# A refitted static order, DMAs begun from ScalarE's queue, and a rebuilt end in an FFT, MLP and soft-MoE kernel

## Chip, cores and metric

One Trainium2 chip, one core. The metric is the device time of one execution in microseconds; three runs of the kernel before took 1426.42, 1427.17 and 1430.96 us, median 1427.17.

## What is computed

Input `x` is 8 batches of 3072 tokens by 256 numbers, float32. Cut to what matters:

```python
X = np.fft.fft(np.fft.fft(x, axis=1), axis=2).real      # per batch, 3072 x 256
h = X.reshape(-1, 256) @ w_in                           # 256 -> 2048
y = (h - np.tanh(h)) @ w_out                            # 2048 -> 256
logits = y @ phi                                        # 32 slots, all 24576 tokens
d = softmax(logits, axis=0)                             # over the tokens
slot_in = d.T @ y                                       # 32 x 256
slot_out = [relu(slot_in[e] @ w1[e]) @ w2[e] for e in range(8)]   # 4 slots an expert
out = softmax(logits, axis=1) @ slot_out                # 24576 x 256
```

The softmax over tokens needs every token's logits, so no output can be written before the last batch is through: the kernel has a loop over the input and then an end, in which the experts run and 25.17 MB of output are made and stored.

## The kernel before

**Loop.** A batch is 12 tiles, and a tile is 4 groups of 512 of the 2048 hidden columns: 96 tiles, 384 groups. For each batch a part of the Fourier transform over tokens is done by additions on 128x1024 pieces of `x` (`dft24`, additions at L327, on GpSimd but for the first batch, scalings at L331 on ScalarE). These run while the batch before goes through the rest, so the loads of batch b (`load_x`, L306, eight DMAs a batch) have to come a batch ahead. For each tile `z_dft` (L411 to L414) finishes the transform on TensorE. For each group, in this order: `wide` (L462) makes two results `pp` and `qq` with three matmuls each, called a pass here; `evac` (L476) and `plus` (L481) on VectorE and `minus` (L484) on GpSimd put them together to h of two mirrored rows; ScalarE makes tanh (`act_h`, L489) and a scaled half-precision copy (`act_t`, L497); VectorE makes the low half (`low_t`, L501); a DMA transposes both (`turn_t`, L505), issued by SyncE (SP); TensorE multiplies the transposed pieces `tt` to `logits` (L532, 16 matmuls) and the untransposed ones to `slots` (L640, 24 matmuls a tile). Every two tiles `ls_sum` (L544) makes logits, which `ls_keep` (L551, SP) stores to `lsd` in DRAM for the end, and a running softmax scales what is summed in `acc` (`acc_add`, L644).

**What sets the order.** Class `Flow` (L112) is a list planner that runs when the program is built. Every operation is entered with a cost on its engine (V VectorE, A ScalarE, G GpSimd, T TensorE, D the DMA queue of SP), what it reads and writes, and the ring of buffers that it takes or frees; the planner then fixes one order for each engine. Entries are sorted by a due place, which `SCHED` gives for every kind of operation in groups (L46), and an engine looks at the next 40 of its entries. The transposes are entered with 2.4 on SP and 2.0 more until they land:

```python
        put(g + 0.001, {"D": 2.4}, lambda e, g=g: turn_t(g), [("t1", g, 0), ("t1", g, 1)], [("tt", g)], "tt", "", 2.0, "low_t1")
```

On the chip nothing is reordered: an engine that waits for a semaphore holds all that is behind it, and a DMA is issued in its place in the instruction stream of the engine that starts it. Before, SP starts all of them.

**Head.** `w_in` and `w_out` come as raw 64-bit halves in 16 pieces of 512 KB (`load_w`, L760). VectorE puts each together in six steps, the last one an addition (`join`, L797). When all are there `top_1` (L884, reduction at L886) finds the largest of w_out times phi, whose scale everything behind needs.

**End.** `late` constants and weights: `wo_unit` (L1055), `wl_unit` (L1067, w1 of experts 6 and 7), `lt_unit` (L1062, logits of four batches), `w128_unit` (L1073, constants `ct` and `wwd`), `t_unit` (L1080, w2, into the ring `tr` of the transposes' sources, 16 DMAs at L1050). Then the sum is normalized (`norm`, `a_norm`), `slot_in` (L1337), the experts' `up` (L1375) and `down` (L1388), `place` and `placed` to `R`; and for each batch a softmax of its logits (`c_max` to `c_div`, L1447 to L1464), twelve transposes `c_t`, twelve products `mix` (L1514), copies to an output buffer `mixed` (L1410 on VectorE, L1412 on ScalarE), and stores.

Of the kernel before, what the change touches and what calls it, by code (L numbers as in the profile page):

```python
# [9 lines left out]
F32 = mybir.dt.float32  # L10
# [216 lines left out]
def fft_mlp_softmoe_kernel(ctx: ExitStack, tc: tile.TileContext, x, w_in, w_out, phi, w1, w2, cq, fd, cm, ct, out):  # L227
# [67 lines left out]
    def load_x(b, cgs=(0, 1), sets=(0, 1, 2)):  # L295
        xb = xbs[b % 2]
        xr = x[b].rearrange("(j p) d -> p j d", p=128)
        for cg in cgs:
            for a in sets:
                c = 4 * cg  # L300
                while c < 4 * cg + 4:
# [4 lines left out]
                    ny.dma_start(out=xb[:, 8 * a + c:8 * a + c + n, :], in_=xr[:, j:j + 3 * (n - 1) + 1:3, :])  # L306
# [3 lines left out]
    tA = tmp.tile([128, 4, 256], F32, name="tA")  # L310
    tB = tmp.tile([128, 4, 256], F32, name="tB")
# [448 lines left out]
    def load_w(dst, src, a, u):  # L760
# [828 lines left out]
```

## Time and profile before

| | us |
|---|---|
| runs | 1426.42, 1427.17, 1430.96 |
| profiled execution | 1421.73 |
| its span on the core | 1419.9 |
| TensorE busy | 1284.0 (90% of the span) |
| VectorE busy | 1241.7 (87%) |
| ScalarE busy | 1132.4 (80%) |
| GpSimd busy | 1126.9 (79%) |
| chain that ended last: DMA `tt<-tr` | 28% |

The span runs from the first to the last instruction of the core; the profiled execution's own time has 1.8 us around it. Shares of busy time are means over head, loop and end, so they are read by stretch. The chain that ended last is followed back from the last instruction, at each step to what released it.

### The profile page before, as it was taken

The numbers are of one execution on the slowest core, as the hardware profiler recorded it, in microseconds if no ns is written. First come the engines' busy times: TensorE is split into PE (matmuls) and PEld (weight loads), VectorE is DVE, ScalarE is ACT, GpSimd is POOL, SyncE is SP. The second block draws the span as 40 slices with busy tenths as digits, with TensorE's granted clock in tenths as the row PEclk, the third lists the DMA queues.
The fourth block names the chain that finished last, engine by engine and source line by source line (L and its number), as shares of the span: only waits on it lengthen the run. The fifth ranks groups of instructions, "written<-read, shape, count | busy, mean of one in ns | idle before, by whom it ended". The sixth has DMA issues, their size and how long they took to land.

```text
span 1419.9 us, 37237 instructions
## 1 busy us (share of the span) xinstructions
PE 1284.0 (90%) x14062; PEld 936.3 (66%) x14062; DVE 1241.7 (87%) x2233; ACT 1132.4 (80%) x2522; POOL 1126.9 (79%) x864
## 2 busy tenths in 40 slices
PE   3889999999899999999999999899989999995886
PEld 2666776667676766677776677676767667762464
DVE  7989898989999999999999999899989989992572
ACT  3459887988888888888898889788988888881476
POOL 5957898999999999999999999899999964430420
PEclk9999999999999999999999999999999999996998
DMA  7469999999999999999999999999999999999778
GB/s 237 149 184 201 200 189 190 180 200 182 207 198 182 196 200 198 188 193 198 207 198 185 194 206 191 188 189 204 185 197 194 213 193 203 189 205 309 238 316 372
DMA packets 856867, 292.84 MB, mean 206 GB/s; under 512 B 803440, under 2 KB 847344, under 8 KB 854896
## 3 DMA queue, kind: packets, MB, share of 16 engines
q1 hardware_dynamic: 856688, 290.47, 104.1%
q8 instruction: 110, 1.80, 0.5%
q14 instruction: 69, 0.57, 0.1%
HBM read 58.15 MB, written 30.67 MB: 63 GB/s over the span
## 4 chain that ended last, share of the span: by engine, by line
PE 58%; DMA 30%; DVE 5%; POOL 2%; issue 2%; ACT 2%; SPq 0%; DVEq 0%; ACTq 0%
DMA tt<-tr 28%; PE pp L462 13%; PE qq L462 12%; PE L L532 9%; PE ta L640 8%; PE op L1514 3%; POOL h L484 1%; PE L L525 1%; PE zps L411 1%; PE zps L412 1%; PE zps L413 1%; PE zps L414 1%; PE hps L838 1%; PE tps L450 1%; PE L L526 1%
## 5 line engine op out<-in xcount | busy, mean ns | idle before, releaser
L484 POOL TENSOR_TENSOR h<-pb,h 128x512 f32<-128x512 f32 x384 | 493.7, 1289 | 146.3 <-DVE h L481 120.8
L489 ACT ACTIVATE th<-h 128x512 f32<-128x512 f32 x768 | 462.2, 613 | 96.8 <-DVE h L481 72.5
L501 DVE SCALAR_TENSOR_TENSOR tr<-th,tr 128x512 f16<-128x512 f32 x768 | 510.5, 682 | 3.2 <-ACT tr L497 3.0
L497 ACT ACTIVATE tr<-th 128x512 f16<-128x512 f32 x768 | 446.0, 607 | 6.7 <-issue 1.3
L462 PE MATMUL pp<-Wh,zh 128*128 128x512 f32 x768 | 335.6, 437 | 0.1
L462 PE MATMUL qq<-Wh,zh 128*128 128x512 f32 x768 | 329.9, 430 | 0.1
L476 DVE SCALAR_TENSOR_TENSOR pb<-W,zts,pp 128x512 f32<-128x512 f32 x384 | 284.3, 741 | 40.9 <-PE pp L462 37.8
L532 PE MATMUL L<-WPn,tt 128*128 128x64 f16 (+1 forms) x6144 | 231.0, 185 | 67.8 <-DMA tt<-tr 66.5
L532 PEld LDWEIGHTS <-tt 128*128 128x128 f16 x6144 | 194.4, 96 | 144.4 <-DMA tt<-tr 105.6
L481 DVE SCALAR_TENSOR_TENSOR h<-pb,qq 128x512 f32<-128x512 f32 x384 | 260.3, 678 | 15.0 <-PE qq L462 6.8
L462 PEld LDWEIGHTS qq<-Wh,zh 128*128 128x128 f32 x768 | 146.2, 190 | 55.6 <-issue 9.1
L462 PEld LDWEIGHTS pp<-Wh,zh 128*128 128x128 f32 x768 | 148.9, 194 | 20.8 <-DVE pb L476 0.7
L327 POOL TENSOR_TENSOR xb<-xb 128x508 f32<-128x508 f32 (+3 forms) x102 | 144.0, 1423 | 18.5 <-DVE xb L327 14.1
L462 PE MATMUL qq<-Wl,zh 128*128 128x512 f32 x384 | 153.5, 400 | 0.0
L462 PE MATMUL pp<-Wl,zh 128*128 128x512 f32 x384 | 152.5, 397 | 0.0
L640 PE MATMUL ta<-tr,dh 128*32 128x512 f16 x2304 | 145.9, 390 | 0.0
L327 POOL TENSOR_TENSOR tA<-xb 128x1024 f32<-128x1024 f32 (+2 forms) x70 | 106.2, 1522 | 1.6 <-ACT xb L331 1.2
L640 PEld LDWEIGHTS <-dh 128*32 128x32 f16 x2304 | 55.9, 98 | 72.1 <-issue 23.4
L327 POOL TENSOR_TENSOR xb<-tA 128x508 f32<-128x508 f32 (+2 forms) x79 | 83.5, 1063 | 0.1
L327 POOL TENSOR_TENSOR xb<-xb,tA 128x512 f32<-128x512 f32 (+1 forms) x46 | 75.9, 1651 | 9.3 <-DVE xb L327 8.6
L462 PEld LDWEIGHTS qq<-Wl,zh 128*128 128x128 f32 x384 | 74.0, 193 | 5.6
L462 PEld LDWEIGHTS pp<-Wl,zh 128*128 128x128 f32 x384 | 73.9, 192 | 1.3
(256 smaller groups left out, 1886.2 us busy)
## 6 DMA issues: line engine op xcount, KB each, us to landing
out<-xb SPq DMA_DIRECT2D x14, 1536.0 KB, 5.4
xb<-in_x SPq DMA_DIRECT2D x32, 512.0 KB, 5.3
tr<-in_moe_w SPq DMA_DIRECT2D x16, 512.0 KB, 9.5
tt<-tr SPq DMA_TRANSPOSE x385, 5.0
xb<-in_moe_w SPq DMA_DIRECT2D x12, 512.0 KB, 4.7
raw<-in_moe_w_in SPq DMA_DIRECT2D x8, 512.0 KB, 4.2
xb<-in_x SPq DMA_DIRECT2D x16, 256.0 KB, 4.1
raw<-in_moe_w_out SPq DMA_DIRECT2D x8, 512.0 KB, 3.6
```

The lines of the kernel that those rows point to most:

```text
L327: fn = lambda e: e.tensor_tensor(out=out[1](), in0=a[1](), in1=c[1](), op=op)
L411: nt.matmul(zps[:, 0, :], xb[:, U, 0:128], C, start=True, stop=False)
L462: nt.matmul(o, z, v, start=n == 0, stop=n == 2)
L476: nv.scalar_tensor_tensor(out=pb, in0=W128[:, c, :], scalar=zs[i][3][:, 129:130], in1=pqs.pop((g, 0)), op0=ALU.mult, op1=ALU.add)
L481: nv.scalar_tensor_tensor(out=hs[g][:, 0, :], in0=pbs[g], scalar=0.5, in1=pqs.pop((g, 1)), op0=ALU.mult, op1=ALU.add)
L484: ng.tensor_tensor(out=hs[g][:, 1, :], in0=pbs.pop(g), in1=hs[g][:, 0, :], op=ALU.subtract)
L489: ns.activation(out=o, in_=hs[g][:, k, :], func=AF.Tanh)
L497: ns.activation(out=place_t(g)[:, 0, k], in_=ths[g, k], func=AF.Copy, scale=T14)
L501: nv.scalar_tensor_tensor(out=t[:, 1, k], in0=ths.pop((g, k)), scalar=T14, in1=t[:, 0, k], op0=ALU.mult, op1=ALU.subtract)
L532: nt.matmul(L[:, pm].rearrange("p b s -> p (b s)")[:, 0:n], tt[:, hl, pm, f, :], WPn[:, 4 * c + f].rearrange("p b s -> p (b s)")[:, 0:n], ...
L640: nt.matmul(tas[p][32 * c:32 * c + 32, :], dhl[p][:, dl, 2 * k + pm, :], ts[c][:, tl, pm, :], start=(k == 0 and n == 0), stop=(i == tiles( ...
L1514: nt.matmul(o.rearrange("p r d -> p (r d)"), c[:, j, :], R[:, 3 * h + k:3 * h + k + 2, :].rearrange("p r d -> p (r d)"), start=(h == 0), s ...
```

## The change

It has four parts.

**Order of the loop.** The due places are other numbers; a transpose is entered with 2.8 and 2.4 instead of 2.4 and 2.0.

**Queues.** The loads of `x` for batches 1 to 7 and the 48 stores of logits are started by ScalarE (`ns`) and not by SP (`ny`). `soft_e` no longer waits for the store, but for the last pair.

**Head.** Eight of the 16 `join`s, those of `w_out` (`apart`), run on GpSimd; the first part of `dft24(0)` runs on GpSimd alone; the loads stand in another order.

**End.** `tA` and `tB`, the scratch of `dft24`, come from the pool of weights and take the constants `ct` and `wwd` when the last transform is done (`const_unit`). w1 of experts 6 and 7 go where `cqs` and `Wl` were. Of the logits only batch 0's are loaded ahead of w2, the softmax of batch 0 is done in the main flow, batches 1 to 3 are loaded behind w2. The sum is not normalized ahead of `slot_in`, but its result is scaled when it is copied to `si`. Products take one of 8 banks each (`room`). `R` is made from PSUM straight. Output buffers are four (two of `xbs`, two pieces of `tr`) where they were two, and the planner gets a tolerance for lateness for each operation of the end (`TL`), and starts from the state in which the main flow ends.

```diff
-DSTEPS = 22.767
-XLEAD = -9.594
-XSTEP = -9.498
-XEARLY = 39.387
-XFIRST = 9.894
+DSTEPS = 12.326
+XLEAD = 6.384
+XSTEP = 1.383
+XEARLY = 15.709
+XFIRST = 26.17
 SCHED = {
-    "soft_t": 14.318, "logits": 5.085, "slots": 17.012, "soft_d": 14.96, "z_slots": 17.04, "z_turn": -1.424,
+    "soft_t": 13.814, "logits": 5.849, "slots": 16.458, "soft_d": 14.952, "z_slots": 17.162, "z_turn": -0.253,
...
-                    ny.dma_start(out=xb[:, 8 * a + c:8 * a + c + n, :], in_=xr[:, j:j + 3 * (n - 1) + 1:3, :])
+                    (ns if b else ny).dma_start(out=xb[:, 8 * a + c:8 * a + c + n, :], in_=xr[:, j:j + 3 * (n - 1) + 1:3, :])
...
     def ls_keep(p):
         b, n = divmod(2 * p, NQ)
-        ny.dma_start(out=lsd_of(b)[:, 2 * n:2 * n + 4, :], in_=lsw[p])
+        ns.dma_start(out=lsd_of(b)[:, 2 * n:2 * n + 4, :], in_=lsw[p])
...
         def join(_):
-            nv.tensor_tensor(out=vf, in0=vf, in1=Y.pop(("f", u)), op=ALU.add)
+            f, lo = Y.pop(("f", u)), tt_.pop(u)[:, :, 0]
+            if u in apart:
+                ng.tensor_tensor(out=vf, in0=vf, in1=lo.bitcast(F32), op=ALU.add)
+            else:
+                nv.tensor_tensor(out=vf, in0=vf, in1=f, op=ALU.add)
...
+    tt_, apart = {}, {("wo", c, k) for c in range(4) for k in range(2)}
...
-    x_part(1)
     hf.add({"D": 1.0}, load_fd, w=["fds"], lat=2.0)
     hf.add({"A": 0.6}, start, ["fds", "cms"], ["fdz"])
-    w_units(units[1:2])
+    w_units(units[1:3])
+    x_part(1)
+    w_units(units[3:5])
     x_part(0)
-    w_units(units[2:])
+    w_units(units[5:])
...
-            hf.add({"V": 0.15 + 0.267 * n, "G": 0.19 + 0.55 * n}, lambda e, fn=fn: fn(vg[e]), r, w, port="V")
+            hf.add({"G": 0.17 + 0.53 * n}, lambda e, fn=fn: fn(vg[e]), r, w)
...
-            put(p0 - XEARLY + 3 * n if n < 3 else p0 + XSTEP * (n - 3), {"D": 1.1}, lambda e, b=b, cg=cg, a=a: load_x(b, (cg,), (a,)), (), ks, "", "",
-                3.5, late=LATES.get("XLEAD", 0.0))
+            put(p0 - XEARLY + 3 * n if n < 3 else p0 + XSTEP * (n - 3), {"A": 0.65}, lambda e, b=b, cg=cg, a=a: load_x(b, (cg,), (a,)), (), ks, "", "",
+                5.0, late=LATES.get("XLEAD", 0.0))
...
-        put(g + 0.001, {"D": 2.4}, lambda e, g=g: turn_t(g), [("t1", g, 0), ("t1", g, 1)], [("tt", g)], "tt", "", 2.0, "low_t1")
+        put(g + 0.001, {"D": 2.8}, lambda e, g=g: turn_t(g), [("t1", g, 0), ("t1", g, 1)], [("tt", g)], "tt", "", 2.4, "low_t1")
...
-        put(8 * p, {"D": 0.75}, lambda e, p=p: ls_keep(p), [("ls", p)], [("lk", p)], "", "", 2.0, "ls_keep")
+        put(8 * p, {"A": 0.4}, lambda e, p=p: ls_keep(p), [("ls", p)], [("lk", p)], "", "", 2.0, "ls_keep")
...
+    early = [(wo_unit, (k,), 1.38) for k in range(4)] + [(lt_unit, (0,), 1.0), (w7_unit, (1,), 1.38)]
+    early += [(w1_part, (6, 0), 1.38), (w1_part, (6, 1), 1.38), (w7_unit, (0,), 1.38)]
...
-    fl = Flow({"cs": 2, "ct": 2, "o": 4, "t": 2, "ot": 2})
+    fm = fl
+    fl = Flow({"cs": 2, "ct": 2, "B": 8, "ot": 4}, 80)
...
-    fl.add({"A": 0.4}, lambda _: ns.copy(out=si, in_=X.pop("b")), ["sip"], ["si"])
+    fl.add({"A": 0.4}, lambda _: ns.activation(out=si, in_=X.pop("b"), func=AF.Copy, scale=rs), ["sip", "rs"], ["si"], free="B:sip")
...
+    for b in range(1, NL):
+        fl.add({"D": 1.0}, lambda _, b=b: lt_unit(b), ["w2s"], [("l", b)], lat=2.0)
...
+    ots = [*xbs, *(tr[:, k:k + 6, :].bitcast(F32).rearrange("p a (b d) -> p (a b) d", d=256) for k in (1, 9))]
...
-            X["ot", b] = xbs[b % 2]
+            X["ot", b] = ots[b % 4]
```

**SP in the loop, before** (L505 is the transpose, L306 a load of x, L551 a store of logits):

```order
L505 DMA_TRANSPOSE tt<-tr 128x16x128 x2
L306 DMA xb_75<-in_x 128x3x256
L306 DMA xb_75<-in_x 128x256
L306 DMA xb_75<-in_x 128x4x256
L505 DMA_TRANSPOSE tt<-tr 128x16x128 x5
L306 DMA xb_75<-in_x 128x4x256
L505 DMA_TRANSPOSE tt<-tr 128x16x128
L551 DMA lsd_57<-lsw 128x128
L505 DMA_TRANSPOSE tt<-tr 128x16x128 x8
```

In the changed program SP has `L508 DMA_TRANSPOSE tt<-tr 128x16x128 x299` there in one row, with no other DMA between. What left it stands on ScalarE, between tanh (L492) and scaled copies (L500), **ScalarE in the loop, after**:

```order
L500 ACTIVATE tr<-th 128x512
L492 ACTIVATE th<-h 128x512
L434 COPY z_4703<-zps 128x256
L492 ACTIVATE th<-h 128x512
L500 ACTIVATE tr<-th 128x512
L310 DMA xb_76<-in_x 128x4x256
L500 ACTIVATE tr<-th 128x512
L457 COPY zts<-tps 128x256
L492 ACTIVATE th<-h 128x512
```

The load stands between two halves of `act_t`; before, ScalarE's order held no DMA.

**TensorE around the logits of group 101, before.** The pass on `qq_6462` is the second of group 106, `tt` is group 101's transpose:

```order
L462 MATMUL qq_6462<-Wh_84,zh_6225 128x512
L462 MATMUL qq_6462<-Wl_85,zh_6225 128x512
L462 MATMUL qq_6462<-Wh_84,zh_6225 128x512
L532 LDWEIGHTS tt_6319
L532 MATMUL L_6174<-WPn_114,tt_6319 128x64
```

Logits follow the pass at once.

**TensorE there, after**, where the same pass writes `qq_6451`:

```order
L465 MATMUL qq_6451<-Wh_84,zh_6240 128x512
L465 MATMUL qq_6451<-Wl_85,zh_6240 128x512
L465 MATMUL qq_6451<-Wh_84,zh_6240 128x512
L414 MATMUL zps_6461<-cqs_113,xb0_75 128x128
L415 MATMUL zps_6461<-cqs_113,xb0_75 128x128
L416 MATMUL zps_6461<-cqs_113,xb0_75 128x128
L417 MATMUL zps_6461<-cqs_113,xb0_75 128x128
L465 MATMUL pp_6471<-Wh_84,zh_6240 128x512
L465 MATMUL pp_6471<-Wl_85,zh_6240 128x512
L465 MATMUL pp_6471<-Wh_84,zh_6240 128x512
L535 LDWEIGHTS tt_6329
L535 MATMUL L_6183<-WPn_114,tt_6329 128x64
```

Four matmuls of `z_dft` and the first pass of group 107 (`pp_6471`) stand now between the two, where before the logits followed at once.

**SP at the end, before** (`lt` logits, `wlw` w1 of 6 and 7, `w128w` constants, `tr` w2). Behind the last transposes stand first three of four loads of logits, all four of `wot` (the product of weights that `slot_in` reads) and one of `wlw`, then:

```order
L1047 DMA wlw<-in_moe_w 128x1024
L1065 DMA lt_22162<-lsd_57 128x768
L1047 DMA wlw<-in_moe_w 128x1024 x2
L1076 DMA w128w<-in_ct 128x608
L1050 DMA tr<-in_moe_w 128x4x256 x2
L1078 DMA w128w<-wwd 128x512
L1050 DMA tr<-in_moe_w 128x4x256 x6
L699 DMA lsd_58<-sls 1x32
L1050 DMA tr<-in_moe_w 128x4x256 x8
```

w2 stands behind the constants and all of the early logits.

**SP at the end, after** (`ltw` holds logits and a piece of w1, `cqs` w1):

```order
L508 DMA_TRANSPOSE tt<-tr 128x16x128 x8
L1074 DMA wot<-wod 128x1024
L1085 DMA ltw<-lsd_57 128x768
L1059 DMA cqs<-in_moe_w 128x1024
L1074 DMA wot<-wod 128x1024 x3
L1079 DMA ltw<-in_moe_w 128x1024
L1059 DMA cqs<-in_moe_w 128x1024
L1079 DMA cqs<-in_moe_w 128x1024
L1062 DMA tr<-in_moe_w 128x4x256 x8
L702 DMA lsd_58<-sls 1x32
L1062 DMA tr<-in_moe_w 128x4x256 x8
L1085 DMA ltw<-lsd_57 128x768 x3
```

The constants left this place (they are loaded among the last batch's transposes), and three of the four loads of logits stand behind w2.

## Rows read from the trace of the kernel before

**Rows 1.** Stretch of the loop: us, busy (and number) of L640's matmuls, then weight loads.
```profile
386.30:1129.10 742.80, 90.23 (x1440) 33.94 (x1440) 1.00 1.12 195
```

**Rows 2.** Stretches of loop, output: us; busy PE, PEld, DVE, ACT, POOL; PEclk, DMA share, GB/s.
```profile
386.30:1129.10 742.80, 700.96 (x8203) 515.80 (x8202) 688.09 (x1236) 641.47 (x1451) 694.28 (x530) 1.00 1.12 195
...
1343.50:1419.90 76.40, 57.11 (x271) 42.95 (x271) 39.41 (x80) 54.47 (x109) 13.16 (x10) 0.95 0.81 330
```

**Rows 3.** Waits from 386.3 to 1129.1: total us, times, longest us.
```profile
PEld L532 <- DMA tt<-tr: 68.7, 81, 3.1
ACT th L489 <- DVE h L481: 47.5, 69, 2.2
...
PEld L532 <- issue: 21.9, 80, 0.3
```

**Rows 4.** By source line: SP's issues (ns min/median/max), then DMA to landing.
```profile
L505 SPq DMA_TRANSPOSE tt<-tr x384: 1316/2516/5780, 95.8 to 1285.5; - x192
...
DMA to landing us min/median/max: 4.2/5.0/8.0
...
L306 SPq DMA_DIRECT2D xb<-in_x x64: 419/623/2371, 1.7 to 973.0; - x64
...
L551 SPq DMA_DIRECT2D lsd<-lsw x48: 320/576/1377, 127.8 to 1291.3; - x48
...
L1050 SPq DMA_DIRECT2D tr<-in_moe_w x16: 378/1367/2717, 1300.5 to 1325.5; - x16
...
DMA to landing us min/median/max: 7.9/9.5/10.4
```

**Rows 5.** SP's timeline near 400 us: start us, us, what, how many.
```profile
405.09 21.93 SPq L505 DMA_TRANSPOSE tt<-tr  x8
```

**Rows 6.** Chain of waits at the end: start us, us, what; then VectorE's `acc`.
```profile
1285.49 4.44 DMA tt<-tr
...
1293.13 8.28 DMA lt<-lsd
...
1312.90 3.64 PE sip L1342 x32
...
1336.61 3.59 PE sop L1392 x64
...
1343.54 1.67 PE op L1514 x6
...
1300.97 0.75 DVE L644 SCALAR_TENSOR_TENSOR acc<-acc,fac,ta 128x512 f32<-128x512 f32 x1 [4.02 <-PE ta L640]
```

**Rows 7.** The same chain in the loop, one pass of three matmuls.
```profile
408.74 0.70 PE pp L462 x3
```

**Rows 8.** VectorE in the head: two groups, L327 alone by stretch, the reduction `top_1`.
```profile
L798 DVE TENSOR_TENSOR tr<-tr,hps 128x512 f32<-128x512 f32 x16 | 10.9, 679 | 0.1
...
L327 DVE TENSOR_TENSOR tA<-xb 128x1024 f32<-128x1024 f32 x1 | 1.2, 1227 | 0.4 <-DMA xb<-in_x 0.4
...
5.40:78.20 72.80, 7.23 (x5) 59.55 (x45) 0.98 0.52 176
...
82.02 0.69 DVE L886 TENSOR_REDUCE am<-tr 128x1 f32<-128x512 f32 x1 [3.73 <-ACT tr L830]
```

**Rows 9.** GpSimd in the head: L327 by stretch (DVE, POOL busy), one large addition.
```profile
14.50:54.71 40.21, 3.61 (x2) 36.92 (x26) 0.96 0.54 187
...
22.08 2.35 POOL L327 TENSOR_TENSOR tA<-xb 128x1024 f32<-128x1024 f32 x1
```

**Rows 10.** Stretches with loads alone and with stores alone: last number is GB/s.
```profile
1300.00:1334.00 34.00, 21.92 (x218) 10.55 (x210) 10.53 (x20) 9.52 (x18) 9.16 (x7) 0.80 1.05 353
1411.00:1418.00 7.00, 0.00 (x0) 0.00 (x0) 0.00 (x0) 0.00 (x0) 0.00 (x0) 0.61 1.00 421
```

**Rows 11.** Groups of the output, 1343.5 to 1419.9.
```profile
L1410 DVE COPY xb<-op 128x512 f32<-128x512 f32 x22 | 15.0, 690 | 22.5 <-PE op L1514 22.5
...
L1456 ACT ACTIVATE h<-h,desc 128x768 f32<-128x768 f32 x2 | 1.9, 964 | 0.0
```

More of the change, by code (lines that the diff above doesn't have):

```diff
@@ L1259, in fft_mlp_softmoe_kernel @@
+    for k, (fn, e, c) in enumerate(C5):
+        put(4 * NT + 7 + 0.1 * k, {e: c}, lambda _, fn=fn: fn(0), [("l", 0)] + tkey(tB), [("l", 0)], late=0.3)
     late = [(t_unit, (n // 2, n % 2)) for n in range(16)]
@@ L1305, in total @@
     def total(_):
-        X["a"] = ps1.tile([128, 1], F32, tag="a", name="rsp")
+        X["a"] = room("ss", 1)
         for r in range(0, 128, NS):
@@ L1335, in clear, with slot_z @@
         ng.memset(R.bitcast(F32), 0.0)
+    def slot_z(_):
+        o = X["b"] = room("sip", 256)
+        for k in range(2):
+            nt.matmul(o[0:32, :], zz[:, k, :], WW[:, k, :], start=(k == 0), stop=False, tile_position=(0, 0))
     def slot_in(_):
-        o = X["b"] = ps1.tile([128, 256], F32, tag="b", name="sip")
+        o = X["b"]
         for j in range(4):
@@ L1388, in down @@
     def down(eg):
-        o = X[eg] = ps.tile([128, 256], F32, tag="o", name="sop")
+        o = X[eg] = room(("sop", eg), 256)
         for f in range(8):
@@ L1393, in down, with place, high, low @@
                           start=(f == 0), stop=(f == 7), tile_position=(0, 32 * r))
[L1395 to L1406 removed]
+    def place(eg):
+        if eg == 0:
+            X["b"] = room("stp", 256)
+        nt.matmul(X["b"], perm[eg], so[eg], start=(eg == 0), stop=(eg == 1))
+    def high(k, h):
+        ns.copy(out=R[h:h + 64, k, :], in_=X["b"][h:h + 64, :])
+    def low(k, h):
+        nv.tensor_tensor(out=R[h:h + 32, 3 + k, :], in0=X["b"][h:h + 32, :], in1=R[h:h + 32, k, :].bitcast(F32), op=ALU.subtract)
     def cp_out(e, out, in_):
@@ L1439, in fft_mlp_softmoe_kernel @@
-            fl.add({"V": 0.62, "A": 0.5}, lambda e, k=k: cp_out(e, hT[k[0]][:, 4 * k[1]:4 * k[1] + 4, :], X.pop(k)),
-                   [("hTp", k)], [("hT", k)], free="t")
-        fl.add({"T": 3.6}, lambda _, eg=eg: down(eg), [("hT", (eg, 0)), ("hT", (eg, 1))] + [("w2", a) for _, a in late[EARLY:] if a[0] // 4 == eg] + ["behind"], [("sop", eg)], take="o")
-        fl.add({"A": 0.4}, lambda _, eg=eg: ns.copy(out=so[eg], in_=X.pop(eg)), [("sop", eg)], [("so", eg)], free="o")
-    fl.add({"T": 0.9}, place, [("so", 0), ("so", 1)], ["stp"])
@@ L1468, in sides @@
+        fl.add({"T": 3.6}, lambda _, eg=eg: down(eg), [("hT", (eg, 0)), ("hT", (eg, 1))] + [("w2", a) for _, a in late if a[0] // 4 == eg],
+               [("sop", eg)], take=B("sop", eg))
+        fl.add({"A": 0.4}, lambda _, eg=eg: ns.copy(out=so[eg], in_=X.pop(eg)), [("sop", eg)], [("so", eg)], free=B("sop", eg))
+        fl.add({"T": 0.6}, lambda _, eg=eg: place(eg), [("so", eg)] + ["stp"] * eg, ["stp"], take="" if eg else "B:stp")
     def sides(cs):
@@ L1563, in fft_mlp_softmoe_kernel @@
                    free="ot" if h else "", lat=2.0)
-    fl.run()
+    experts(0)
+    combine(0)
+    combine(1)
+    experts(1)
+    for k, h in ((0, 0), (1, 64), (2, 0)):
+        fl.add({"A": 0.42}, lambda _, k=k, h=h: high(k, h), ["stp", "R0"], [("R", k)])
+        fl.add({"V": 0.46}, lambda _, k=k, h=h: low(k, h), ["stp", ("R", k)], [("R", 3 + k)], free="B:stp" if k == 2 else "")
+    for b in range(2, NB):
+        combine(b)
+    for b in range(NB):
+        put_out(b)
+    fl.run(fm)
 _INS = ["x", "moe_w_in", "moe_w_out", "moe2_phi", "moe2_w1", "moe2_w2"]
```

286 lines of the change are left out of this document (139 added, 147 removed).

## The prediction, written before the changed kernel ran

> **What bounds the kernel now.** Read the table of stretches first. From 386.3 to 1129.1 us the kernel is in its repeating state; the 1440 matmuls of `slots` [rows 1] at 24 a tile make that 60 tiles, 12.38 us each. In the same 742.80 us GpSimd is busy 694.3, VectorE 688.1, ScalarE 641.5 [rows 2]: per tile 11.57, 11.47 and 10.69. So no engine is idle by more than 0.8 to 1.7 us a tile, and the one with the least room is GpSimd (48.5 us idle), then VectorE (54.7).
>
> The table of waits of that stretch says who is late. TensorE's weight loads for `logits` wait 68.7 us in 81 places for the transpose of tanh (`tt<-tr`), and 21.9 us more right behind it as "issue": 90.6 us, 1.51 us a tile, by far the largest wait of TensorE [rows 3]. ScalarE waits 47.5 us for `plus`: it gets its data late because TensorE was late.
>
> Then the queue that issues the transposes. One takes 2.5 us of SP (median, 1.3 to 5.8) and 5.0 us to land (4.2 to 8.0) [rows 4]. In a burst eight went in 21.93 us, 2.74 each [rows 5]. Four a tile are 11.0 us of 12.38: SP's line is nearly full too. The loads of x cost it 0.62 us a piece, the stores of logits 0.58 [rows 4].
>
> Last the head and the end. In the head VectorE is the line that everything waits in. At the end no batch is left to hide anything: the last transpose is issued at 1285.5, the first product of the output starts at 1343.54 [rows 6], and the rest to 1419.9 is output.
>
> The profiled run took 1421.73 us (span 1419.9), 5.4 below the median of 1427.17. The sum is made on the profiled run; the forecast is the median plus the sum.
>
> **The loop: -28 us (between 0 and -68).** Three edits meet here.
> (a) SP loses 7 x 8 load pieces of x and 48 stores. Per batch 8 x 0.62 + 6 x 0.58 = 8.4 us of 148.6 leave the line in which the transposes stand [rows 4]. The bytes stay: the DMA engines carry the same traffic.
> (b) The refitted order puts one more pass of three matmuls (0.70 us in the chain [rows 7]) between the second pass of a group and its `logits`: 11 instead of 10 in nearly all groups (289 and 283 of 310 that I counted), beside a little more of `slots`, some 1.0 us of TensorE work in all. The mean wait in a place where TensorE waits is 68.7 / 81 = 0.85 us [rows 3]. Taken alone, 1.0 us of further cover would remove nearly all of the 1.51 us a tile.
> (c) But then the others must keep up. GpSimd has 0.81 us a tile to give, over the 84 tiles that share it with the next batch's transform 68 us: that is the far bound. The near bound is nothing. I take 0.3 us a tile, 96 x 0.3 = 28, nearer to nothing, because GpSimd at 93.5% (694.3 / 742.8), VectorE at 92.6% and SP's line at about 89% (11.0 of 12.38) all have to be met by one fixed order, and what TensorE no longer waits for shows next as VectorE waiting for `pp`, and transposes queueing for the DMA engines.
>
> The Trainium skill speaks against (a): in "DMA: Bandwidth & Descriptors", section "Issuing engines are not separate DMA queues", DMAs of all queues run on the same 16 engines and interleave, so that a second issuer saves the sequencer's issue time alone. By that rule (a) is worth at most its 8.4 us of SP a batch and nothing in transfer time. No DMA of this kernel starts from ScalarE in the trace, so it can't show it.
>
> ScalarE gets what SP loses: 56 loads and 48 stores, 13 a batch. At SP's prices that is 7.8 us a batch, where ScalarE idles (742.8 - 641.5) / 5 = 20.3 us [rows 2]: I cost it at nothing, hidden in that idle time. Its price there isn't in the trace. The nearest rows are SP's: 0.32 us at the least, 2.4 at the most for a load of x, 1.4 (median) to 2.7 for loads issued into a full queue [rows 4]. I take 0.6, the row of the same transfers; the upper end is a rival below. Behind a load that has to wait for its rows of x the tanh work of ScalarE waits too.
>
> **The head: -5 us (0 to -8).** VectorE works through 16 weight pieces until 82.02 - 3.73 = 78.3 us [rows 8]. Eight of the 16 last additions go to GpSimd, 8 x 0.68 = 5.4 us; five additions of the first transform leave too, 7.23 us [rows 8]. But four large additions of 1.2 us come back to VectorE ahead of `top_1` (4.9 us): the gain is 7.7 us, if GpSimd is on time. On GpSimd, what now stands ahead of its last addition of a weight is what ran there from 14.5 to 54.71 (36.9 us busy), eight additions of 128x512 at half of a 1024's 2.35, and the five, four of them that large: 36.9 + 9.4 + 10.6 = 56.9 [rows 9]. VectorE would be done at 78.3 - 7.7 = 70.6, so GpSimd has to begin by 13.7 us and never wait. Before, it began at 14.5 and waited 3.3. The nearer end is the gain, because only the last addition is waited for; a few us late leave 5. Nothing is the other end.
>
> **The end: -17 us (-5 to -20).** Up to the first product: before, the normalization waits for constants that are queued behind other loads; the chain shows 8.28 us of DMA, and `slot_in` starts at 1312.90 [rows 6]. They now land during the loop, so `slot_in` starts after `acc` (1300.97 + 0.75 = 1301.7 [rows 6]) and not 11 us later. That alone moves `up` forward by 8 us, but the second `down` needs the last weights: the last of 16 loads of w2 is issued at 1325.5 [rows 4] and lands 9.5 later, 1335.0, and the second `down` starts at 1336.61 [rows 6]. So what counts is the bytes in front. Before, 28.1 pieces of 512 KB stand between the last transpose and that landing (4 wot, 4 wlw, 16 w2, 3.0 of logits, 1.1 of constants); now 24.75, 1.75 MB less, at 353 GB/s [rows 10] 5.0 us. The landing comes at 1330.0, `down` is ready there instead of 1.6 us later, and from its start to the first product, 6.9 us before, goes a copy of 0.4: together -7.
>
> The output itself is 25.17 MB. Before, it takes 76.4 us, at 330 GB/s, where the stores alone reach 421 GB/s [rows 2, 10], 59.8 us. What holds it: two output buffers, so a batch's products wait until the batch two before is stored; VectorE's copies wait 22.5 us for TensorE [rows 11]. With four buffers the ring no longer decides. Engines have 54.5 + 39.4 us [rows 2] on ScalarE and VectorE, and 3 x 2 x 0.96 of softmax that before was done ahead (exponentials and sums of three batches, a sum taken at the price of an exponential [rows 11]): 100 us, 50 on each. So the stores become the bound: 59.8, 1.2 ahead of the first, 2 for the last landing, 63. I leave 3 for the second batch, whose logits now land only behind the weights: 66.4, -10. The 5 us of bytes ahead of it alone are one end; 63 us (-13) and the 7 the other.
>
> Sum: -28 - 5 - 17 = -50 on 1421.7; on the median **1377**.
>
> **The rivals.**
> *The loop gives nothing.* The sequencer's time on SP is not what the transposes wait for: the bytes and the order of engines' work are the same, and GpSimd and SP's line were nearly full: the wait for `tt` only moves. For it: a transpose takes 5.0 us to land where SP spends 2.5 on it [rows 4], and the DMA engines' busy share in the loop is 1.12 [rows 2], so transfers overlap on them. Against: one pass more of cover is in the order, and 81 waits of 0.85 us are just of its size. 1427 - 22 = 1405. This is how the section of the Trainium skill's page named above would have it for part (a).
> *GpSimd is filled.* Waits for `tt` vanish and GpSimd runs at 100%: -68 instead of -28, 1337. Against: three lines above 90%.
> *Slower: ScalarE is held by the DMAs it starts.* If a start on ScalarE takes as long as one into a full queue, 2.4 us [rows 4], 13 a batch are 31 us where 20.3 are idle: +10.7 a batch, +86 in all, 1427 - 22 + 86 = 1491. It decides from (20.3 + 22 / 8) / 13 = 1.8 us a start on; at 2.0 it would be 1451. Against: SP's median is 0.62 with transposes in flight all the time.
> *The four output buffers don't do what is said*, since two of them hold w2 until `down` is done: the end gives 7 alone, 1387, inside the forecast's range.
>
> **How the numbers follow.** The forecast has 0.57 (1358 to 1396, a loop between -10 and -45 beside head and end at their bounds; the last rival lies in it); loop gives nothing 0.24 (1398 to 1412); GpSimd filled 0.08; ScalarE held 0.11. The range 1345 to 1412 leaves out the last two, 0.19. About 0.3% is what runs of this kernel can tell from no change. Slower by more is the third rival at 0.08; within 0.3% it needs a start of some 1.8 us, 0.03 of the same rival; the other three are faster, 0.89.
>
> **What would show it.** Right: a tile of 12.1 us between the same two batches; the wait of `logits` for `tt` well under 1.0 us a tile; ScalarE's issues of `xb<-in_x` at 0.4 to 0.8 us; `top_1` at 77; the first product some 51 us behind the last transpose's issue (58 before); output in 66 us at 375 GB/s or more. Wrong: ScalarE's issues over 1.5 us with tanh late; GpSimd or VectorE idle as before; stores that wait for copies.

## The result and the profile after

The changed kernel took 1389.91 us (median of 4 runs, 1385.48 to 1394.80) against 1427.62 for the kernel before; the ratio is 0.9731, with a 95% interval of 0.9700 to 0.9762. The forecast was 1377, the range 1345 to 1412. The profiled execution took 1385.48 us, its span is 1383.7.

The stretches of the profile after answer to [rows 2]; the columns are the same. Batches 2 to 6, the last batch up to its last pass, from the last transpose to the first product, and the output:

```profile
372.70:1098.60 725.90, 703.00 (x8218) 519.89 (x8216) 685.99 (x1236) 643.79 (x1448) 694.54 (x532) 0.99 1.14 197
1098.60:1247.30 148.70, 144.41 (x1661) 102.69 (x1661) 138.00 (x251) 125.32 (x274) 73.15 (x61) 1.00 1.12 206
1261.00:1311.40 50.40, 35.22 (x389) 17.75 (x385) 10.89 (x24) 13.17 (x32) 9.09 (x7) 0.80 1.01 330
1311.40:1383.70 72.30, 56.74 (x275) 45.64 (x275) 49.16 (x91) 49.46 (x101) 30.09 (x25) 0.91 0.86 349
```

Sixty tiles took 725.9 us where they took 742.8: 12.10 in place of 12.38 us a tile. The waits of that stretch (total us, times, longest) answer to [rows 3]:

```profile
PEld L535 <- issue: 37.8, 110, 0.4
PEld L535 <- DMA tt<-tr: 29.7, 23, 3.8
ACT th L492 <- DVE h L484: 22.4, 28, 3.4
```

The wait of the logits for the transposes fell from 68.7 us in 81 places to 29.7 in 23. The "issue" behind a wait rose from 21.9 to 37.8: together 67.5 in place of 90.6 us, 1.12 for 1.51 us a tile. GpSimd is busy 694.5 of 725.9, 95.7%.

The lines of the issues, by queue (ns min/median/max) and landing, answer to [rows 4]. ACTq is ScalarE's sequencer:

```profile
L508 SPq DMA_TRANSPOSE tt<-tr x384: 1316/2554/7367, 100.6 to 1261.0; - x192
...
DMA to landing us min/median/max: 4.3/5.2/11.5
...
L310 ACTq DMA_DIRECT2D xb<-in_x x56: 374/391/2157, 77.8 to 944.3; - x56
L310 SPq DMA_DIRECT2D xb<-in_x x8: 433/753/1588, 3.6 to 12.8; - x8
...
L554 ACTq DMA_DIRECT2D lsd<-lsw x48: 326/345/368, 127.3 to 1267.1; - x48
```

A start on ScalarE costs 0.39 us for a load of x and 0.35 for a store of logits, less than on SP (0.62 and 0.58 [rows 4]).

Where the 36.2 us of span went, from the first `wide` pass of each batch, the last transpose's issue, and the first product on the chain of waits:

| stretch, us | before | after | difference |
|---|---|---|---|
| start to the first pass | 81.5 | 78.1 | -3.4 |
| batches 0 and 1 | 304.8 | 294.6 | -10.2 |
| batches 2 to 6 | 742.8 | 725.9 | -16.9 |
| batch 7 to its last transpose's issue | 156.4 | 162.4 | +6.0 |
| from there to the first product | 58.1 | 50.4 | -7.6 |
| output | 76.4 | 72.3 | -4.0 |

So the loop is worth 21.1, the end 11.6 and the head 3.4. The chain of waits at the end, against [rows 6]:

```profile
1260.95 4.83 DMA tt<-tr
...
1283.40 6.68 DMA lsd<-sls
...
1304.34 3.63 PE tps L1444 x64
...
1311.37 5.31 PE tps L1538 x15
```

The second `down` starts 43.4 us behind the last transpose's issue, where it were 51.1, and the first product 50.4 behind it. The output is no longer held by a buffer. Its chain from 1335 on is TensorE alone; three pieces of it:

```profile
1341.32 1.31 PE tps L1510 x12
1342.63 5.67 PE tps L1538 x24
1348.30 1.31 PE tps L1510 x12
```

The 24 matmuls of a batch's twelve products take 5.67 us and the twelve transposes of the next batch 1.31: 7.0 us a batch. What the stores carry shows where time is lost all the same (last column GB/s):

```profile
1316.00:1321.00 5.00, 4.25 (x24) 3.12 (x23) 4.39 (x8) 4.51 (x8) 2.42 (x4) 1.00 1.02 342
1321.00:1326.00 5.00, 4.87 (x21) 3.72 (x22) 4.79 (x11) 4.02 (x9) 3.81 (x4) 1.00 0.51 176
1326.00:1331.00 5.00, 5.00 (x29) 4.10 (x28) 4.65 (x11) 4.21 (x10) 3.12 (x3) 1.00 0.57 236
1331.00:1336.00 5.00, 4.88 (x27) 3.94 (x27) 4.74 (x8) 4.79 (x10) 2.66 (x3) 1.00 0.99 418
...
1371.00:1376.00 5.00, 0.00 (x0) 0.00 (x0) 0.00 (x0) 0.00 (x0) 0.00 (x0) 0.78 1.02 430
```

Up to 1321 the first batch is stored, one DMA a pair of rows. Between 1321 and 1331 the stores run at half of their rate: the second batch's logits land behind w2, its softmax is late, and its store waits for all twelve products. From 1331 to 1376 the DMA engines are full.

### The profile page after: what moved, and what is told of

The parts are those of the page before. It is cut to its first block, busy times and chain, and to the rows that moved or that the text cites. A ratio compares the mean times of both kernels' runs of the same rounds, so it can differ in the third digit from the quotient of the medians.

```text
span 1383.7 us, 37153 instructions
## 1 busy us (share of the span) xinstructions
PE 1285.8 (93%) x14062; PEld 940.5 (68%) x14062; DVE 1235.6 (89%) x2229; ACT 1125.0 (81%) x2512; POOL 1138.1 (82%) x875
## 4 chain that ended last, share of the span: by engine, by line
PE 61%; DMA 16%; POOL 7%; DVE 5%; ACT 5%; issue 3%; SPq 1%; ACTq 0%; DVEq 0%; POOLq 0%
DMA tt<-tr 14%; PE qq L465 14%; PE pp L465 14%; PE L L535 9%; PE ta L643 7%; PE tps L1538 3%; POOL h L487 3%; POOL xb L330 2%; ACT th L492 2%; DVE tr L504 1%; DVE pb L479 1%; DVE h L484 1%; PE tps L453 1%; PE zps L414 1%; ACT tr L500 1%
## 5 line engine op out<-in xcount | busy, mean ns | idle before, releaser
L492 ACT ACTIVATE th<-h 128x512 f32<-128x512 f32 x768 | 457.3, 608 | 80.9 <-DVE h L484 43.1
L500 ACT ACTIVATE tr<-th 128x512 f16<-128x512 f32 x768 | 445.7, 601 | 13.9 <-DVE lsw L547 4.0
L465 PE MATMUL qq<-Wh,zh 128*128 128x512 f32 x768 | 336.3, 438 | 0.7 <-ACT dT L595 0.7
L465 PE MATMUL pp<-Wh,zh 128*128 128x512 f32 x768 | 319.3, 416 | 3.2 <-DVE pb L479 0.9
L535 PEld LDWEIGHTS <-tt 128*128 128x128 f16 x6144 | 198.1, 96 | 110.7 <-issue 58.0
L465 PEld LDWEIGHTS pp<-Wh,zh 128*128 128x128 f32 x768 | 145.3, 189 | 53.4 <-issue 6.7
L330 POOL TENSOR_TENSOR xb<-xb 128x508 f32<-128x508 f32 (+3 forms) x100 | 139.5, 1400 | 6.9 <-DVE tB L330 6.5
L330 POOL TENSOR_TENSOR xb<-tA 128x508 f32<-128x508 f32 (+2 forms) x78 | 83.2, 1075 | 4.8 <-DVE xb L330 4.7
L465 PEld LDWEIGHTS pp<-Wl,zh 128*128 128x128 f32 x384 | 73.3, 191 | 10.2
```

Source lines behind the costliest of these rows:

```text
L330: fn = lambda e: e.tensor_tensor(out=out[1](), in0=a[1](), in1=c[1](), op=op)
L465: nt.matmul(o, z, v, start=n == 0, stop=n == 2)
L492: ns.activation(out=o, in_=hs[g][:, k, :], func=AF.Tanh)
L500: ns.activation(out=place_t(g)[:, 0, k], in_=ths[g, k], func=AF.Copy, scale=T14)
L535: nt.matmul(L[:, pm].rearrange("p b s -> p (b s)")[:, 0:n], tt[:, hl, pm, f, :], WPn[:, 4 * c + f].rearrange("p b s -> p (b s)")[:, 0:n], ...
```

## The experiments

Times are medians; the ratio is to the kernel before on the same chip. Two theories stood against each other for the loop: **order** (the gain is the further pass that covers a transpose) and **queue** (it is SP's line, from which 8.4 us a batch went). Some runs keep the order of TensorE, VectorE and GpSimd and change only who starts a DMA.

**1. The changed kernel, SP starts everything.**

```diff
-                    (ns if b else ny).dma_start(
+                    ny.dma_start(
...
-        ns.dma_start(out=lsd_of(b)[:, 2 * n:2 * n + 4, :], in_=lsw[p])
+        ny.dma_start(out=lsd_of(b)[:, 2 * n:2 * n + 4, :], in_=lsw[p])
```

> The changed kernel with every load of x and every store of logits started by SP again; the order of TensorE, VectorE and GpSimd is the changed kernel's, instruction by instruction, and ScalarE loses its DMA starts alone. Theory order (the loop's gain comes from the refitted order, which gives the transposes more cover): the loop keeps its 12.1 us a tile within 0.1, the time is 1383 to 1393, the lower half because ScalarE no longer starts six loads in a row at 77.8 us in the head. Theory queue (the gain comes from the 8.4 us a batch that left SP's line): SP has 48 x 2.75 + 8.4 = 140 us of some 143 a batch, transposes are late and 15 to 20 us of the loop's 21 go back: 1400 to 1412.

Measured: 1408.45 us, ratio 0.9848 (0.9814 to 0.9882). 18.5 us of the 37.7 went back (17 by the ratios); the head and the end, whose orders are the same, took 77.7 us to the first pass and 50.6 + 72.5 behind the last transpose, so it is the loop. Whole-run waits of its weight loads for the transposes (51.2 us in 45 places in the changed kernel):

```profile
PEld L535 <- DMA tt<-tr: 76.3, 66, 4.0
```

The queue theory's number came out, on this order.

**2. The kernel before, ScalarE starts them.** The reverse edit on the old order.

> The kernel before with the same loads and stores started by ScalarE; the order of TensorE, VectorE and GpSimd is that of before. Theory order: no change or a few us, 1420 to 1430, and 12.3 to 12.4 us a tile. Theory queue: 15 to 20 us less, 1407 to 1413, and 12.1 to 12.2 us a tile.

Measured: 1426.39 us, ratio 0.9988 (0.9958 to 1.0019): nothing. Here the order theory's number came out; the interval reaches from 6 us less to 3 more. The same waits were 105.6 us in 119 places on the old queue, and now:

```profile
PEld L532 <- DMA tt<-tr: 94.1, 101, 4.7
```

**3. The kernel before, one pass more of cover, ScalarE's queue.**

```diff
-    "logits": 5.085
+    "logits": 5.849
-    "ls_sum": 12.386
+    "ls_sum": 12.994
-    "ls_keep": 12.495
+    "ls_keep": 13.103
```

> The kernel before with the loads of x and stores of logits started by ScalarE, and with the due place of the logits moved from 5.085 to 5.849 (the sum and the store of logits moved with it): eleven passes between a group and its logits in 263 of 310 groups, where it were ten in 283. Nothing else is refitted. Theory cover (the one pass more is what the loop gains from): waits of logits for the transposes fall by half or more, a tile takes 12.1 to 12.2 us, 1405 to 1415. Theory fit (it takes the whole refit, cover alone only moves the wait): a tile stays at 12.3 to 12.4, 1420 to 1430.

Measured: 1408.43 us, ratio 0.9893 (0.9868 to 0.9918): 15 us less than before by the ratio, 17 by the medians, with three due places moved (two of them to the refit's numbers) and the queue. The time is what the cover theory gave; the tile is not (12.27 in the profile), nor did the waits halve:

```profile
PEld L532 <- DMA tt<-tr: 74.4, 79, 3.9
```

**4. The same order, SP starts everything.**

> The kernel before with the due place of the logits moved (eleven passes in place of ten) and SP starting all DMAs as before: TensorE, VectorE and GpSimd have, instruction by instruction, the order of the run with cover and ScalarE's queue, which took 1408.4. Theory both (cover and queue need one another: a queue alone gave nothing on the old order, and SP's line gave back 18 us on the new one): 1418 to 1426. Theory cover alone: 1406 to 1412.

Measured: 1418.70 us, ratio 0.9930 (0.9904 to 0.9956): 9 to 10 us less than before; ScalarE's queue adds 5 us by the ratios, 10 by the medians, with intervals that just overlap. The time lies at the edge of what the theory "both" gave: cover alone gains, but far less than the theory of cover alone said. That the queue adds to it beyond the noise is shown on the refitted order alone (run 1). In its profile the gain lies in batches 0 and 1 (296.6 us for 304.8); batches 2 to 6 stayed at 12.38 a tile, and of their 90.6 us of waits 81.1 are left:

```profile
PEld L532 <- DMA tt<-tr: 53.3, 48, 2.8
...
PEld L532 <- issue: 27.8, 100, 0.5
```

How far one profile's tile can be trusted is seen in the seven profiles that have the changed kernel's order and queue up to the end (the profile after and runs 7 to 12): their batches 2 to 6 take 720.1 to 731.8 us, 12.00 to 12.20 a tile. The clock that TensorE was granted differs between them (third number from the right, a share of 2.4 GHz). The shortest and the longest, runs 8 and 12, and then runs 2 and 4:

```profile
380.30:1100.40 720.10, 700.69 (x8217) 517.18 (x8216) 685.41 (x1236) 643.61 (x1448) 694.17 (x532) 1.00 1.15 199
378.00:1109.80 731.80, 707.28 (x8217) 521.99 (x8215) 685.97 (x1237) 644.50 (x1448) 694.17 (x531) 0.98 1.14 195
...
389.40:1132.40 743.00, 705.61 (x8203) 520.77 (x8202) 687.57 (x1236) 639.69 (x1451) 694.02 (x530) 0.98 1.13 195
...
378.00:1120.90 742.90, 704.18 (x8203) 529.66 (x8202) 686.28 (x1236) 641.98 (x1451) 694.40 (x531) 0.98 1.10 195
```

At 0.98 TensorE is busy some 3 to 7 us longer with the same matmuls than at 1.00, which the kernel before had [rows 2]. So the 12.38 of runs 2 and 4 may hide a gain of some microseconds; that a queue or a pass alone leaves the tile where it was is not shown by them.

The six kernels can be read side by side. From the records of each profile, the means over the transposes of groups 60 to 323, in us: how long a transpose waits for SP after its source is ready (`late`), from SP's start to landing (`land`), and from the source to landing. The last two are over the three in four whose landing is on record.

| order, starter | time | late | land | source to landing |
|---|---|---|---|---|
| old, SP (before) | 1427.6 | 1.84 | 5.27 | 7.16 |
| old, ScalarE | 1426.4 | 1.24 | 5.66 | 6.91 |
| one pass more, SP | 1418.7 | 2.02 | 5.23 | 7.30 |
| one pass more, ScalarE | 1408.4 | 1.54 | 5.68 | 7.22 |
| refitted, SP | 1408.5 | 2.83 | 5.31 | 8.17 |
| refitted, ScalarE (after) | 1389.9 | 1.79 | 5.64 | 7.43 |

Taking the other DMAs from SP shortens `late` by 0.5 to 1.0 us, and lengthens `land` by 0.33 to 0.45; that the moved transfers now meet the transposes on the DMA engines would explain it, but no run shows it. From the source to landing that leaves 0.25 us of gain on the old order, 0.08 with one pass more, and 0.74 on the refitted one, where the wait for SP was the longest (2.83). So the means go with the large gain of the refitted order, but not with the rest: 0.25 went with no change of the time and 0.08 with 5 to 10 us. The refit did one more thing that the forecast did not see: from a group's second pass to its last `low_t` it takes 6.99 us in place of 7.54, which one pass more of cover alone does not change (7.54 and 7.60).

**5. The kernel before with the whole new loop, old head and end.** All due places, the transposes' planner costs and the queue, nothing else.

> The kernel before with the whole of the change to the loop (all due places, the transposes' planner costs, ScalarE's queue) and with its own head and end. Theory: the parts add up, the loop is worth 21 us and a tile takes 12.1: 1404 to 1410. Rival: part of the gain in the loop hangs on the head and the end being planned with it, or the old end takes some back (its loads stand behind transposes that are late): 1411 to 1420.

Measured: 1414.04 us, ratio 0.9930 (0.9907 to 0.9953): 10 to 12 us less, not 21, and not better than run 3. In its profile batches 0 and 1 take 309.3 us, 14.7 more than after, and batches 2 to 6 12.24 a tile; but that execution took 1424.61 us, 10.6 above the median of the ten. The same due places gave half of their gain with the old head and end. Which of them is at odds with the old head was not followed.

**6. The changed kernel, old head.** All `join`s on VectorE (`apart` empty), the first transform shared as before, the old order of loads.

> The changed kernel with the head of before: all sixteen last additions on VectorE, the first part of the transform shared by VectorE and GpSimd, the loads in the old order. The planner starts the loop from another state, so the loop's order differs too. Theory: the head is worth 3 to 5 us, `top_1` comes at 82, 1393 to 1396. Rival (the gain at `top_1` is lost again before the first transposes, which were issued at 100.6 after and 95.8 before): 1385 to 1391.

Measured: 1400.97 us, ratio 0.9814 (0.9774 to 0.9853): 11 us more than after. The first reduction starts at 81.43, so 2.4 of it lie in the head; batches 0 and 1 take 304.2 us for 294.6, with an order of the loop that the planner laid out anew. Batches 2 to 6 keep 12.08 a tile, so the loop's gain there does not hang on the new head. Head and order are not separated in the first two batches.

**7. The second batch of x started by SP.** The edit is `ns if b > 1` for `ns if b`. In the profile after, ScalarE starts six loads in a row right where the chain passes:

```profile
77.83 5.36 ACTq L310 DMA_DIRECT2D xb<-in_x  x6
83.24 0.37 ACT L444 CAST zh<-zps 128x256 fp32r<-128x256 f32 x1 [5.14 <-issue]
```

> The changed kernel with only the eight loads of the second batch of x (the first that ScalarE starts) on SP. Theory held: the six starts in a row that take ScalarE 5.36 us at 77.83, while the chain waits for its next copy, are on the path: the main part begins 3 to 5 us earlier and the time is 1385 to 1387. Theory free: ScalarE's start lies beside VectorE's scale computations, which end at 85 anyway: within 1 us of the changed kernel, 1389 to 1391.

Measured: 1391.05 us, ratio 0.9731 (0.9700 to 0.9763): the theory that this holds the head falls. The scale for the logits is ready 4.4 us after the reduction's start where it was 4.95.

**8. The last batch's loads started by ScalarE.** In the last batch transposes stand in SP's line one behind the other (SP's timeline after: start, us, how many):

```profile
1226.19 13.68 SPq L508 DMA_TRANSPOSE tt<-tr  x4
...
1240.61 22.54 SPq L508 DMA_TRANSPOSE tt<-tr  x8
```

```diff
-        ny.dma_start(out=w1s[e][:, k, :], in_=w1[e, 128 * k:128 * k + 128, :])
+        (ns if e < 6 else ny).dma_start(out=w1s[e][:, k, :], in_=w1[e, 128 * k:128 * k + 128, :])
```

and the two loads of constants likewise.

> The changed kernel with the 12 loads of w1 and the two of constants that stand among the last batch's transposes started by ScalarE; TensorE, VectorE and GpSimd keep their order. Theory line (in the last batch SP's line is what all waits for: transposes wait there up to 10.8 us after their source is ready): 14 starts of 0.58 us, 8 us, leave it; the last transpose is issued 5 to 8 us earlier and the time is 1382 to 1385. Theory engines (transposes take 2.8 us each because the DMA engines carry everything, whoever starts it): 0 to 2 us less, 1388 to 1390.

Measured: 1386.23 us (1381.29 to 1392.36), ratio 0.9738 (0.9693 to 0.9782), the same as the changed kernel's. The last batch took 163.2 us to its last transpose's issue, for 162.4. With SP's line free of other DMAs:

```profile
1205.37 60.35 SPq L508 DMA_TRANSPOSE tt<-tr  x19
```

19 in 60.35 us are 3.18 each, and before the edit 16 in the three last bursts after 1213 took 2.96 each. So SP's line in the last batch is not full because of the other starts that SP makes; the transposes themselves are taken at that pace, with the DMA engines' share at 1.12 there. What sets the pace was not tested.

**9. Two output buffers.**

```diff
-    fl = Flow({"cs": 2, "ct": 2, "B": 8, "ot": 4}, 80)
+    fl = Flow({"cs": 2, "ct": 2, "B": 8, "ot": 2}, 80)
...
-            X["ot", b] = ots[b % 4]
+            X["ot", b] = ots[b % 2]
```

> The changed kernel with two output buffers in place of four; nothing else changes, up to the last products. Theory ring (the buffers are what the output gains from): batch 2 waits for batch 0's stores and every later one for the batch two before, as in the kernel before, some 8.2 us a batch in place of 7.0: 5 to 8 us longer, 1395 to 1398. Theory late batch (the output is held by the second batch's late logits and then by stores at full rate): 0 to 2 us longer, 1390 to 1392.

Measured: 1393.76 us, ratio 0.9751 (0.9713 to 0.9789). In its profile the output takes 80.6 us for 72.3, 8.3 more, as the ring theory has it; the time is only 3.9 longer, inside the intervals, and the first product came 2 us sooner behind the last transpose in that profile. From the last transpose's issue to the end of the span it is 129.1 us for 122.7; in runs 7, 8 and 12, which change nothing or only a store there, 121.1 to 122.5. Waits of its output that the changed kernel does not have:

```profile
ACT xb L1462 <- DMA out<-xb: 6.3, 1, 6.3
DVE xb L1460 <- DMA out<-xb: 5.7, 1, 5.7
```

**10. The second batch's logits ahead of the last eight pieces of w2, and its store in pairs.** The load goes ahead in SP's list; the store is that of run 11.

> The changed kernel with the second batch's logits loaded ahead of the last eight pieces of w2 and with the second batch stored in pairs of rows as the first is, not in two halves. Theory hole (the output loses its time between 1316.7 and 1331, where the second batch waits for its softmax and its store for all twelve products): 4 to 7 us less, 1383 to 1386, although the second `down` waits 1 us longer for its weights. Theory TensorE (7.0 us a batch of products and transposes set the pace): within 1 us of the changed kernel, 1389 to 1391.

Measured: 1398.43 us, ratio 0.9822 (0.9790 to 0.9854): 8.5 us slower than the changed kernel, and neither theory's number. In its profile 8.8 of 16.1 us more lie ahead of the last transpose's issue, where the order is the changed kernel's, so those do not come from the edit; behind it the end takes 130.1 us for 122.7. The planner laid out the softmaxes in another order, and in the middle of the output TensorE waits for a row of them on VectorE, in the chain of waits:

```profile
1341.37 1.66 DVE tB L1097 x2
1343.04 0.87 DVE tB L1107
...
1344.97 2.17 DVE cs L1504 x2
...
1347.18 1.54 PE tps L1511 x6
```

**11. The second batch stored in pairs alone**; no engine's order but SP's changes.

```diff
-        if b == 0:
+        if b < 2:
...
-        for h in range(2 if b else 0):
+        for h in range(2 if b > 1 else 0):
```

> The changed kernel with the second batch of the output stored in twelve pairs of rows, as the first is, and not in two halves when all twelve are there; nothing but SP's stores changes. Theory hole (the DMA engines carry 176 and 236 GB/s from 1321 to 1331 because the second batch's store waits for its last product, and stores at full rate behind it end last): 3 to 5 us less, 1385 to 1387. Theory pace (products at 7.0 us a batch end the kernel): 0 to 1 us less, 1389 to 1390.

Measured: 1387.01 us (6 runs, 1380.67 to 1393.54), ratio 0.9708 (0.9671 to 0.9744), which overlaps the changed kernel's interval. The hole is filled, but at another rate, and a shorter one opens behind it, before the third batch's halves:

```profile
1322.00:1327.00 5.00, 4.94 (x26) 3.82 (x25) 4.62 (x11) 3.71 (x8) 3.48 (x3) 1.00 1.00 341
1327.00:1332.00 5.00, 5.00 (x27) 4.00 (x25) 4.85 (x12) 4.64 (x11) 3.26 (x3) 1.00 1.02 341
1332.00:1337.00 5.00, 4.88 (x28) 3.96 (x27) 4.73 (x10) 4.75 (x11) 2.61 (x3) 1.00 0.66 256
1337.00:1342.00 5.00, 5.00 (x30) 4.18 (x28) 4.42 (x8) 4.38 (x8) 3.92 (x4) 1.00 1.03 433
```

Stores in pairs move 341 GB/s with the DMA engines busy throughout, stores in halves 433. SP starts a pair of 262144 bytes every 0.77 us there, which is the same rate; that the engines set it and not SP is read from their share of 1.00 to 1.02 alone. The output takes 71.2 us for 72.3, but the first product came 1.1 later, and from the last transpose's issue to the end it is 122.7 us in both. So the lower median is not shown to come from the end.

**12. The last batch in pairs too.**

> The same with the last batch stored in pairs too. Theory hole: with the queue of stores shorter by what the second batch gained, the last pair is started right behind the last copy, not both halves: another 2 to 4 us, 1381 to 1385, and the span ends 6 to 9 us after the last product where it were 14.5. Theory pace: as the second batch alone. If twelve starts of 0.65 us a batch hold SP longer than the halves did: no gain, or a loss of 1.

Measured: 1393.54 us, ratio 0.9738 (0.9699 to 0.9778): no gain. The span ends 15.5 us after the last product, for 14.6. No run beat the changed kernel beyond the intervals.

## Why the prediction was right, and where it was off

**The loop, -28 forecast, -21 measured.** Part (b) held in its direction: one pass more of cover is worth 10 us with SP's queue and, with ScalarE's, 15 beside a queue that alone gave nothing that could be measured (runs 2 to 4, by the ratios). Its size did not hold. "Nearly all of the 1.51 us a tile" was to go by cover alone, and 1.35 stayed in run 4 (81.1 / 60) and 1.12 in the changed kernel. Part (c), 0.3 us a tile, was a choice, and it is 16.9 / 60 = 0.28 in batches 2 to 6; that it came so near is partly luck, since one profile's tile varies by 0.1. The step that failed is the "96 x 0.3": the first two batches gave 10.2 where 24 x 0.3 are 7.2, and the last one took 6.0 more where it should have given 3.6. There GpSimd has no next batch (busy 73.15 of 148.7 us), and the transposes are late: from group 336 on they wait 6.1 us for SP in the mean, for 1.8 before. They come at 3.0 to 3.2 us each whoever starts the loads beside them (run 8). The last one is issued 7.4 us behind its source, for 3.3: that is 4.1 of the 6.0, and the passes ahead of it take 148.7 us for 147.1. Why the old order's last batch was 6 us shorter with the same loads of w1 is not settled. The new due places alone are not the cause, since in run 5 it takes 157.5; the two loads of constants, which moved into it, are only 0.57 MB, 1.6 us at the rate of [rows 10].

**The queue.** Part (a) was left at "at most 8.4 us of SP a batch", inside the sum. It is worth 17 to 18.5 us (at most 2.3 a batch) on the refitted order, 5 to 10 with one pass of cover and nothing that could be measured on the old one. The Trainium skill's rule, in "DMA: Bandwidth & Descriptors", section "Issuing engines are not separate DMA queues", holds as to what happens: transfers started from two engines interleave, and each transpose landed 0.33 to 0.45 us later. That section also calls the sequencer's time usually small beside the DMA itself; here SP spends 2.55 us on a transpose that lands in 5.2, and what else stood in its line decided nearly half of the gain (run 1). The rival that took the rule to its end, a loop that gains nothing, is refuted for the whole change and came true in run 2.

**ScalarE's price**, taken as 0.6 us a start, was 0.39 and 0.35, far from the 1.8 from which the third rival decides; the six starts in a row in the head cost nothing that could be measured (run 7).

**The head, -5 forecast.** `top_1` came at 79.0 for 82.0, and not at 77:

```profile
14.47 2.36 POOL L330 TENSOR_TENSOR tA<-xb 128x1024 f32<-128x1024 f32 x1 [14.03 <-DMA xb<-in_x]
...
73.11 1.28 POOL L803 TENSOR_TENSOR tr<-tr,raw 128x512 f32<-128x512 f32 x1 [0.87 <-DVE raw L798]
...
79.03 0.62 DVE L897 TENSOR_REDUCE am<-tr 128x1 f32<-128x512 f32 x1
```

GpSimd began at 14.47, when x had landed behind two more weights, where 13.7 was the condition. But it is not what was late at the end: its last addition of a weight waited 0.87 us for VectorE's L798. VectorE was to be done at 70.6 and ended that step at 73.03. The step that failed is "only the last addition is waited for". TensorE waits for earlier ones too, and in the profile after its granted clock falls in the middle of one such wait, at 25.5 us. TensorE and VectorE in that profile, then the same groups of TensorE before, then VectorE's wait in run 10:

```profile
26.47 1.54 PE L828 MATMUL hps<-cms,tr 128*128 128x128 f32 x6 [3.76 <-POOL tr L803]
27.80 3.62 PE L880 MATMUL hps<-tr 128*128 128x256 f32 x8
...
37.81 0.69 DVE L859 SCALAR_TENSOR_TENSOR Wl<-hps,Wh 128x512 fp32r<-128x512 f32 x1 [3.59 <-ACT Wh L854]
...
31.96 0.88 PE L817 MATMUL hps<-cms,tr 128*128 128x128 f32 x6 [2.15 <-DVE tr L798]
32.67 1.89 PE L869 MATMUL hps<-tr 128*128 128x256 f32 x8
...
42.56 0.69 DVE L859 SCALAR_TENSOR_TENSOR Wl<-hps,Wh 128x512 fp32r<-128x512 f32 x1 [6.97 <-ACT Wh L854]
```

The same eight matmuls take 3.62 us for 1.89. ScalarE's `Wh`, which is made from TensorE's results, comes late, and VectorE waits for it: from 15 to 62 us 4.9 us in all, for 1.3 before and 8.2 in run 10. The stretch from 20 to 40 us before, after and in run 10 (granted clock third from the right; a mean below 1.00 means that a part of it ran at the lower level, 1.2 in place of 2.4 GHz):

```profile
20.00:40.00 20.00, 16.06 (x62) 10.13 (x63) 18.70 (x32) 8.90 (x19) 17.23 (x11) 1.00 0.44 151
...
20.00:40.00 20.00, 16.24 (x64) 11.46 (x63) 14.37 (x24) 8.25 (x18) 17.52 (x13) 0.83 0.48 163
...
20.00:40.00 20.00, 16.29 (x56) 12.62 (x55) 13.46 (x23) 7.29 (x14) 17.20 (x12) 0.68 0.51 169
```

The eight profiles with the new head show the reduction at 77.6 to 83.9, mean 80.2, and it goes with this clock: 77.6 and 78.7 at 0.91, 79.0 to 80.1 at 0.83, 83.2 and 83.9 at 0.66 and 0.68. The six with the old one have it at 81.4 to 82.6, mean 82.1. So some 2 us are gained in the mean, and the head has become uneven. Both profiles at 83 and more come from one chip (runs 8 and 10), so chip and clock are not separated, and what makes the clock fall is not shown.

**The end, -17 forecast, -11.6 measured.** The first product was to come 51 us behind the last transpose's issue and came 50.4; this term is -7.6 for -7. The output was the term that was mis-sized: -4 for -10. The step was "the stores become the bound", with "3 for the second batch". The buffers act: with two of them, the softmaxes that are now done late make the output 80.6 us (run 9). But TensorE with 7.0 us a batch stands right beside the stores' 7.5 (59.8 / 8), and the second batch's lateness costs not 3 us but, over the two windows from 1321 to 1331 at 176 and 236 of 421 GB/s, 5 x (0.58 + 0.44) = 5.1, and the first batch's pairs cost 5 x 0.19 = 0.9 more in the window before, which had no term. What is left over is the ramp and the last landing. Filling the hole did not bring that back: pairs are stored more slowly, and another hole opened behind (run 11).

The range held, but it says little: it also holds the loop that gives nothing (1405), and it is the tile of 12.10 us and runs 1 to 4 that tell the two apart. The nearest number of all is the fourth rival's 1387, but the reason it gives, buffers that do not act, is not what run 9's profile shows. Two sums of the prediction are off without consequence: 96 x 0.3 is 28.8, and a loop of -10 to -45 with the head's and the end's own bounds gives 1354 to 1412, not 1358 to 1396.

## What to carry to other kernels

A wait of TensorE for a DMA has three parts: the issuing queue's line, the transfer and the cover in the order; what shortening one pays hung here on the others, so test them crosswise (the queue alone gave nothing that could be measured, and 17 to 18.5 us on the refitted order). A term per tile is not to be multiplied by all tiles: first and last batches run beside other work and have other bounds. A list planner's due places are fitted to one program: with another head and end the same numbers gave half. Work moved to a slower engine is waited for wherever its result is read, not only at its last piece.

## What was not expected of the hardware

Stores of two rows each moved 341 GB/s with the DMA engines full, stores of a half of a batch 409 to 433 right behind them in the same kernel (run 11). A DMA start costs ScalarE 0.39 us where the same load costs SP 0.62. The head with eight additions on GpSimd varied by 6 us between profiles at the same instructions, the old one by 1: within a wait of 3.76 us TensorE's granted clock fell from 2.4 to 1.2 GHz, and eight matmuls took 3.62 us for 1.89. In the profile before it did not fall between 20 and 40 us, where TensorE had waits of 2.15 us and, up to 21.62, of 8.44.
